# First loads, low weight bits on ScalarE, and the place of W's products in a fused attention, MoE and MLP kernel

## The chip, the cores and the metric

The kernel runs on one core of one Trainium2 chip. The metric is the device time of one execution in microseconds (us), lower is better; the kernel before was run three times. The engines are TensorE (PE; its weight loads are listed as PEld), VectorE (DVE), ScalarE (ACT), GpSimd (POOL) and SyncE (SP), which here issues most DMAs.

## The reference

Three stages follow each other; shapes are in brackets.

```python
# 1. linear attention with decay, per head [4 batches, 8 heads, 768 steps, 48 dims]
for t in range(S):
    cur   = einsum('bhd,bhe->bhde', u * k_t, v_t)
    y_t   = einsum('bhd,bhde->bhe', r_t, state + cur)
    state = w * state + einsum('bhd,bhe->bhde', k_t, v_t)
# 2. x = y as [3072, 384]; top-1 mixture of 8 experts with a skip score
xc = x[x @ w_skip > 0];  e = argmax(xc @ w_gate);  g = softmax(xc @ w_gate)[e]
x[those rows] = xc + g * (relu(xc @ w1[e]) @ w2[e])          # w1 [384, 1024], w2 [1024, 384]
# 3. second MLP
out = (((x @ m1) * (x @ m2)) @ w3) @ w_out                   # m1, m2 [384, 1024], w3 [1024, 1024], w_out [1024, 384]
```

Stage 3 uses one matrix W = w3 @ w_out, computed once, so that only one product is left after `(x @ m1) * (x @ m2)`. The weights of stage 3 arrive as 64-bit floats.

## The kernel before, in words

**Attention.** The 768 steps are cut into 12 chunks of 64, and the heads of two pairs of batches give 24 tiles `n` (chunk `n // 2`, pair `n % 2`) of 128 partitions. A tile needs two loads: `TB` (`load_t`, r and k transposed, 512 KB) and `KV` (`load_v`, r, k and v, 576 KB). `TB` has three buffers, `KV` two for each pair. Per tile:

- `prep` (line 359, DVE) multiplies `TB` by tables of powers of w and gives `FK`;
- `scores` (line 371, PE, 32 products of 48 rows and 64 columns into the one bank `sc`); `evac` (line 376, DVE) masks them into `Fs`;
- `prep_k` (line 383, POOL) gives `kd` and waits for `prep` of the tile after; `prep_m` (lines 389 and 390, POOL) gives r·u·k, `bonus` (line 395, DVE) sums it and `prep_v` (line 405, ACT, 8 instructions) multiplies v by it;
- `y_mm` (lines 425 and 428, PE, 32 + 32 products of 64 or 48 rows); `x_out` (line 446, DVE) adds the bonus and stores the tile to memory;
- `ds_mm` (line 441, PE, 32 products) adds to the state `S` in PSUM; `state_copy` (lines 413 and 415, DVE and ACT) scales it and copies it to SBUF;
- `x_trans` (line 457) and `logits` (line 470), PE, full array, feed the router, whose steps `route_a` to `route_d` and `place` run on DVE for groups of tiles; `place_mm` (line 599) is PE.

The order is written out by hand: everything from line 733 on is emitted in program order on each engine's queue, and no planner moves it. The loop at line 772 does, for n = 0 to 21: `load_t(n+4)`, `prep(n+2)`, `state_copy(n+1)`, `scores(n+1)`, `prep_k(n+1)`, `prep_m(n+2)`, `evac(n+1)`, `bonus(n+1)`, `y_mm(n)`, logits and transposes of earlier tiles, `x_out(n)`, `ds_mm(n)`, `place_mm`, `load_v(n+4)`, `place`. After it a tail of eleven steps finishes tiles 22 and 23 and the router, gathers the rows of the first expert (`load_x`, line 863) and transposes them (`trans_x`).

**W between the tiles.** The products of W are 64 (8 blocks `f` by 8 `g`, `w_mm`, line 696), each one fp32 product of 128 by 128 by 384, shown in the trace as two instructions of line 708. `keep(k)` takes one product for each 4 units of `k` if its weights are ready; if none is, each 2 units cost one `idle_mm`, two dummy products of bf16 (`DQ` = 256 columns). `WK[n]` gives the units at two places: the first before was after `y_mm`, the second after `x_trans` and `prep_v`, ahead of `ds_mm`. In the tail `TK`, `TQ` and `KW` give them, and the last line of it runs what is left:

```python
        trans_x(0)
        while n_w[0] < NF:
            keep(1)
```

**The weights of W.** `jobs` (line 273) are 12 raw loads of 768 or 1024 KB (`load_w`, three buffers). Each is narrowed from 64 to 32 bits: `magnitude` (line 105, ACT), then `shift` (line 113), `low` (line 116) and `sign` (line 120), all DVE. `w_step` takes the next of these three; `WN[n]` says how many at each of three places in an iteration. A block is usable after three calls of `w_ready`. The first three raw loads are issued ahead of the loop, among `load_v(2)`, `load_v(3)` and `load_t(3)`.

Stages 2 and 3 (from line 908 and line 1082) are not touched.

Of the kernel before, what the change touches and what calls it, by code (L numbers as in the profile page):

```python
# [8 lines left out]
F32 = mybir.dt.float32  # L9
F32R = mybir.dt.float32r  # L10
BF16 = mybir.dt.bfloat16
I32 = mybir.dt.int32
AF = mybir.ActivationFunctionType
ALU = mybir.AluOpType
# [17 lines left out]
BIG = 1.0e6  # L32
WLO, WHI = 0.5, 1.5
DQ = 256
NM, NW = 10, 9
# [7 lines left out]
W3B = 5  # L43
WK = [(1, 1)] * 9 + [(1, 2)] * 13
WN = [(0, 0, 0)] * 2 + [(1, 1, 1)] * 5 + [(1, 0, 1)] * 15
KW = 16
# [13 lines left out]
def fused_kernel(ctx, tc, att, kv, wt, u, wg, we, w3, wo, w12, r, k, v, wu, out):  # L60
# [46 lines left out]

    def narrow(raw, t):

        wl, wh = raw[:, :, 0], raw[:, :, 1]  # L110

        def shift():
            nc.vector.tensor_scalar(out=t, in0=t, scalar1=3, scalar2=None, op0=ALU.logical_shift_left)

        def low():
            nc.vector.scalar_tensor_tensor(out=t, in0=wl, scalar=29, in1=t,
                                           op0=ALU.logical_shift_right, op1=ALU.bitwise_or)

        def sign():
            nc.vector.scalar_tensor_tensor(out=t, in0=wh, scalar=-0x80000000, in1=t,  # L120
                                           op0=ALU.bitwise_and, op1=ALU.bitwise_or)

        return [shift, low, sign]

# [101 lines left out]
    with tc.manual_schedule():  # L226
# [10 lines left out]
        def load_t(n):  # L237
            nc.sync.dma_start(out=TB[n % 3].rearrange("p a h t -> p (a h t)"), in_=att[n])
# [21 lines left out]
        load_t(1)  # L260
        nc.sync.dma_start(out=un.rearrange("p h d -> p (h d)"), in_=u.to_broadcast([P, D]))
        load_v(0)
        load_v(1)
        load_t(2)
        nc.gpsimd.memset(ident, 0.0)
        nc.gpsimd.affine_select(out=ident, in_=ident, compare_op=ALU.not_equal, fill=1.0, base=0,
# [33 lines left out]
        nc.vector.tensor_tensor(out=UT[:, 0, 0], in0=Ur, in1=cb, op=ALU.mult)  # L300
        SB = [ps_s.tile([P, 512], F32, tag=f"S{bp}", name=f"S{bp}") for bp in range(2)]
        S = [b[:, 0:D].rearrange("p (h d) -> p h d", h=NH) for b in SB]

        half = [slice(64 * q, 64 * q + 64) for q in range(2)]
# [79 lines left out]

        def prep_m(n):

            c, bp = divmod(n, 2)
            m = P_[n] = wk.tile([P, NH, HD], F32, name="m")
            first = nc.gpsimd.tensor_tensor(out=m, in0=KV[bp][c % 2][:, 0], in1=un, op=ALU.mult)
            nc.gpsimd.tensor_tensor(out=m, in0=KV[bp][c % 2][:, 1], in1=m, op=ALU.mult)  # L390
            return first
# [167 lines left out]
        found, pend = [], []  # L559
        SL = [b[:, 384:464] for b in SB]  # L560
        for b in SL:
            nc.vector.memset(b, 0.0)
        slots = wk.tile([P, 80], F32, name="slots", bufs=1)
# [72 lines left out]
        w3_ = {}  # L636

        done, fresh = set(), [[], [], []]
        n_w = [0]

        def w_steps():


            def front(i):
# [11 lines left out]
                if wide:  # L656
                    magnitude(raw, x.bitcast(I32))
                    return narrow(raw, x.bitcast(I32))
                return [lambda: nc.scalar.copy(out=x, in_=raw)]

            ops = None
            for i, job in enumerate(jobs):
# [5 lines left out]
                for k, op in enumerate(now):  # L668
                    op()
                    if k + 1 == len(now):  # L670
                        load_w(i + 3)
                        fresh[-1].append(job)
                    if ops is None:
                        ops = front(i + 1)
                    yield
# [58 lines left out]
        table_k(0)  # L734
        load_t(3)
        nc.vector.tensor_tensor(out=UT[:, 1, 1], in0=Tk, in1=cb, op=ALU.mult)
        prep(1)
        sc = scores(0)
        prep_m(0)
        table_k(1)  # L740
        prep_k(0)
        evac(0, sc)
        bonus(0)
        prep_m(1)
        for bp in range(2):
            nc.vector.memset(S[bp], 0.0)
        nc.vector.tensor_tensor(out=w128, in0=pw[:, 5], in1=pw[:, 5], op=ALU.mult)
        prep_v(0)
        more_consts = consts()
        load_w(0)  # L750
        load_v(2)
        load_v(3)
        nc.sync.dma_start(out=wgs, in_=wg)
        load_w(1)
        load_w(2)
        todo = []
# [15 lines left out]
        for n in range(NT - 2):  # L772
# [13 lines left out]
            if n == NT - 3:  # L786
                bonus(NT - 1)
            next(more_consts, None)
            w_step(WN[n][0])
            w_ready()  # L790
            y_mm(n)
            keep(4 * WK[n][0])
            run_todo()
            if n > 0:
                x_trans(n - 1)
            prep_v(n + 1)
            keep(4 * WK[n][1])
            w_step(WN[n][1])
            w_evac(0)
            x_out(n)  # L800
            ds_mm(n)
            place_mm(n % 2)
            if n + 4 < NT:
                load_v(n + 4)
            if n < NT - 3:
                place(3)
# [36 lines left out]
        nc.vector.tensor_tensor(out=fb[:, 0:8], in0=wc, in1=wtt, op=ALU.not_equal)  # L843
        nc.vector.tensor_copy(fb[:, 8:16], acc)
    actx.close()

# [567 lines left out]
def _layout(i):  # L1414
# [20 lines left out]
    def words(a):  # L1435
# [11 lines left out]
        "wt": wt,  # L1447
        "u": c(u.reshape(1, D)),
        "wg": c(wg.reshape(ND, P, 9).transpose(1, 0, 2)),
# [23 lines left out]
```

## Time and profile before

| | us |
|---|---|
| median of 3 runs (lowest, highest) | 633.9 (633.12, 634.04) |
| the profiled execution | 637.01 |
| its span in the trace | 635.3 |
| PE busy, share of the span | 614.5, 97% |
| DVE busy, share of the span | 464.1, 73% |
| ACT busy, share of the span | 290.7, 46% |
| POOL busy, share of the span | 141.3, 22% |

The table gives busy time over the whole span, in which three stages with different limits lie one after the other; attention and the products of W end at about 184 us. A busy PE is not PE at its peak: an instruction that waits for its weights or runs at half clock counts as busy. In rows of the trace, times are from the span's start, "x32" counts instructions, and "[2.24 <-DVE ...]" is idle time of the engine ahead of the row and who ended it.

### The profile page before, as it was taken

Reading aid. Unit: us, or ns where it says so; the run is one execution under the profiler, and the core shown is the slowest. Engines: PE = TensorE matmul, PEld = TensorE weight load, DVE = VectorE, ACT = ScalarE, POOL = GpSimd, SP = SyncE. Lnnn points to the kernel's source line nnn. Section 1 sums busy time; section 2 is a strip of 40 time slices with the busy share of each in tenths; the row PEclk is TensorE's granted clock in tenths of the full one; section 3 lists DMA queues with packets and bytes.
Section 4 is the critical chain, followed back from the end, with each engine's and each line's share of the span. In section 5 each row is a group of like instructions: output and inputs, shape, how many; then the busy total and the mean of one; then the engine's idle time right before and its main releaser. Section 6 shows DMA issues by size and latency. Waiting matters only on the chain.

```text
span 635.3 us, 15258 instructions
## 1 busy us (share of the span) xinstructions
PE 614.5 (97%) x6313; PEld 545.4 (86%) x6313; DVE 464.1 (73%) x820; ACT 290.7 (46%) x705; POOL 141.3 (22%) x140
## 2 busy tenths in 40 slices
PE   7999998999999999999998999999999999999996
PEld 6888877888769999989997989988988988988985
DVE  7699998986477799999956954863863863863760
ACT  2555644534355667666534542443443442442430
POOL 3856465463040232232132300000000000000000
PEclk9799998999999999999999999999999999999999
DMA  8889988575148768877321002002002002000001
GB/s 310 358 280 378 326 291 286 177 252 198 45 127 301 277 230 296 287 241 272 112 75 57 1 17 84 1 18 83 2 18 84 1 17 84 2 18 33 1 2 55
DMA packets 26941, 90.40 MB, mean 142 GB/s; under 512 B 4009, under 2 KB 10729, under 8 KB 25840
## 3 DMA queue, kind: packets, MB, share of 16 engines
q1 hardware_dynamic: 24816, 84.11, 38.1%
q0 software_dynamic: 2048, 5.24, 2.5%
q8 instruction: 51, 0.84, 0.5%
q14 instruction: 26, 0.21, 0.1%
HBM read 77.61 MB, written 12.39 MB: 142 GB/s over the span
## 4 chain that ended last, share of the span: by engine, by line
PE 78%; DVE 11%; DMA 5%; issue 3%; ACT 1%; SPq 0%; POOL 0%; DVEq 0%; ACTq 0%
PE po L1237 16%; PE xy L1196 11%; PE za L1196 10%; PE zb L1196 8%; PE wp L708 6%; PE hp L923 6%; PE y L942 5%; DMA TB<-in_att 3%; DVE elo L87 3%; PE sc L371 3%; PE S L441 2%; PE y L425 2%; PE y L428 1%; PE G L428 1%; DVE hl L927 1%
## 5 line engine op out<-in xcount | busy, mean ns | idle before, releaser
L1178 DVE TENSOR_TENSOR C<-st,za 128x512 f32<-128x512 f32 x47 | 32.3, 687 | 69.7 <-ACT st L1213 69.6
L87 DVE TENSOR_TENSOR elo<-raw,ehi 128x768 fp32r<-128x768 f32 x64 | 60.4, 948 | 4.1 <-ACT ehi L86 4.0
L1237 PE MATMUL po<-pl,W_hi 128*128 128x512 f32 (+1 forms) x152 | 58.1, 383 | 0.0
L1237 PE MATMUL po<-ph,W_hi 128*128 128x512 f32 (+1 forms) x152 | 58.0, 382 | 0.0
L1237 PE MATMUL po<-ph,W_lo 128*128 128x512 f32 (+1 forms) x152 | 57.6, 379 | 0.0
L923 PE MATMUL hp<-xh,ehi 128*128 128x240 f32 x192 | 54.5, 286 | 3.0 <-DVE hl L927 2.4
L1213 ACT COPY st<-xy 128x256 f32<-128x256 f32 x47 | 17.6, 374 | 81.8 <-PE xy L1196 81.8
L86 ACT CAST ehi<-raw 128x768 fp32r<-128x768 f32 x64 | 52.7, 829 | 2.1 <-DMA raw<-in_we 2.1
L1196 PE MATMUL xy<-bxh,w12h 128*128 128x256 f32 x188 | 53.3, 283 | 0.0
L1196 PE MATMUL xy<-bxl,w12h 128*128 128x256 f32 x188 | 53.1, 282 | 0.0
L1196 PE MATMUL xy<-bxh,w12l 128*128 128x256 f32 x188 | 53.1, 282 | 0.0
L923 PE MATMUL hp<-xl,ehi 128*128 128x240 f32 x192 | 52.6, 276 | 0.0
L923 PE MATMUL hp<-xh,elo 128*128 128x240 f32 x192 | 52.4, 274 | 0.0
L708 PE MATMUL wp<-wo_s,w 128*128 128x384 f32 x128 | 51.7, 515 | 0.1
L405 ACT ACTIVATE zv<-KV,z 128x48 f32<-128x48 f32 x184 | 44.0, 327 | 8.0 <-DVE z L395 6.9
L1196 PE MATMUL za<-bxh,w12l 128*128 128x512 f32 x141 | 45.1, 320 | 0.0
L1196 PE MATMUL za<-bxh,w12h 128*128 128x512 f32 x141 | 45.0, 319 | 0.0
L1196 PE MATMUL za<-bxl,w12h 128*128 128x512 f32 x141 | 44.7, 317 | 0.0
L942 PE MATMUL y<-ehi,hh 128*128 128x384 f32 (+1 forms) x128 | 43.3, 339 | 0.0
L942 PE MATMUL y<-elo,hh 128*128 128x384 f32 (+1 forms) x128 | 43.2, 338 | 0.0
L942 PE MATMUL y<-ehi,hl 128*128 128x384 f32 (+1 forms) x128 | 43.1, 337 | 0.0
L923 PEld LDWEIGHTS hp<-xh,ehi 128*128 128x128 f32 x192 | 36.1, 189 | 7.9 <-DVE hl L927 6.9
(249 smaller groups left out, 1671.5 us busy)
## 6 DMA issues: line engine op xcount, KB each, us to landing
raw<-in_we SPq DMA_DIRECT2D x32, 768.0 KB, 5.1
KV<-in_kv SPq DMA_DIRECT2D x24, 576.0 KB, 5.3
TB<-in_att SPq DMA_DIRECT2D x24, 512.0 KB, 7.3
raww<-in_w SPq DMA_DIRECT2D x8, 1024.0 KB, 7.5
raw<-in_w SPq DMA_DIRECT2D x8, 768.0 KB, 6.6
xm<-xg SPq DMA_DIRECT2D x48, 96.0 KB, 3.3
out<-ob SPq DMA_DIRECT2D x17, 256.0 KB, 2.0
x<-xm SPq DMA_DIRECT2D x20, 192.0 KB, 2.8
```

The source lines that it names most:

```text
L86: nc.scalar.copy(out=hi, in_=raw)
L87: (eng or nc.vector).tensor_tensor(out=lo, in0=raw, in1=hi.bitcast(F32), op=ALU.subtract)
L371: nc.tensor.matmul(sc[m, h], FK[d, 1, h], FK[d, 0, h], start=True, stop=True)
L405: nc.scalar.activation(out=zv[:, h], in_=v[:, h], func=AF.Copy, scale=z[:, h:h + 1])
L425: nc.tensor.matmul(yv[m, h], Fs[m, h], v[m, h], start=(h == 0), stop=True, skip_group_check=True)
L708: nc.tensor.matmul(ps, w3[:, g], wo_s[:, g], start=(g == 0), stop=(g == NF - 1))
L923: nc.tensor.matmul(hp, a, b, start=(i == 0), stop=(i == 8))
L942: nc.tensor.matmul(ys[e, t], a[:, P * t:P * t + ROWS[t]], b[:, D:2 * D], start=(f == 0 and i == 0), stop=(f == NF - 1 and i == 2))
L1178: nc.vector.tensor_tensor(out=halves(C[:, 0]), in0=st[:, 0:2], in1=halves(za), op=ALU.add)
L1196: nc.tensor.matmul(o, a, m, start=first and i == 0, stop=(i == 2), skip_group_check=True)
L1213: nc.scalar.copy(out=st[:, 0], in_=X)
L1237: nc.tensor.matmul(po, a[:, f, c], b[:, t], start=(i == 0), stop=(i == 3 * NF - 1))
```

## The change

- **Loads.** `u` is stored 128 times in memory and loaded without a broadcast. `load_v(2)` comes right after `load_t(2)`, `load_v(3)` after `load_t(3)`. The three first raw loads of W leave the start: `load_w(0)`, `(1)` and `(2)` are issued in iterations 1, 2 and 3, after `load_v(n+4)`.
- **Start.** The two PSUM memsets of the state and of the slots become one per bank, at the very start. `prep_m(0)` moves from POOL to DVE, behind `evac(0)`. The constants of the router (`consts`) start at n = 2 and not at n = 0.
- **Low bits.** For W's weights `shift` and `low` are replaced: `ahead` (ACT) turns the low word, read as an unsigned integer, into the three low bits in a tile `bits`; `join` (DVE) shifts and ors in one instruction. `sign` stays. The next job's `magnitude` is issued after a job's last step and not after its first. The weights of stage 3's other matrices (`prep_steps`) keep the three DVE steps.
- **W's steps and products.** `WN` gives no step before n = 3, one at n = 3 and two per iteration from n = 4. The first place of `keep` moves ahead of `y_mm`, directly behind `scores(n+1)`; the second behind `ds_mm` and `place_mm`, directly ahead of the next `scores`. `WK` gives 4 and 0 units for n = 0 to 8, 4 and 4 for n = 9 and 10, 8 and 8 from n = 11.

```diff
-WK = [(1, 1)] * 9 + [(1, 2)] * 13
-WN = [(0, 0, 0)] * 2 + [(1, 1, 1)] * 5 + [(1, 0, 1)] * 15
+WK = [(1, 0)] * 9 + [(1, 1)] * 2 + [(2, 2)] * 11
+WN = [(0, 0, 0)] * 3 + [(0, 0, 1)] + [(1, 0, 1)] * 18
+LW = (1, 2, 3)
...
-        return [shift, low, sign]
+        def ahead():
+            nc.scalar.activation(out=bits, in_=wl.bitcast(U32), func=AF.Copy, scale=LOW[0], bias=LOW[1])
+
+        def join():
+            nc.vector.scalar_tensor_tensor(out=t, in0=t, scalar=3, in1=bits,
+                                           op0=ALU.logical_shift_left, op1=ALU.bitwise_or)
+
+        return [shift, low, sign] if bits is None else [ahead, join, sign]
...
-        nc.sync.dma_start(out=un.rearrange("p h d -> p (h d)"), in_=u.to_broadcast([P, D]))
+        nc.sync.dma_start(out=un.rearrange("p h d -> p (h d)"), in_=u)
         load_v(0)
         load_v(1)
         load_t(2)
+        load_v(2)
+        SB = [ps_s.tile([P, 512], F32, tag=f"S{bp}", name=f"S{bp}") for bp in range(2)]
...
+        for b in SB:
+            nc.vector.memset(b[:, 0:464], 0.0)
...
-                    if ops is None:
+                    if ops is None and k + 1 == len(now):
                         ops = front(i + 1)
...
         load_t(3)
+        load_v(3)
         nc.vector.tensor_tensor(out=UT[:, 1, 1], in0=Tk, in1=cb, op=ALU.mult)
         prep(1)
         sc = scores(0)
-        prep_m(0)
         table_k(1)
         prep_k(0)
         evac(0, sc)
+        prep_m(0, nc.vector)
         bonus(0)
         prep_m(1)
-        for bp in range(2):
-            nc.vector.memset(S[bp], 0.0)
...
-        load_w(0)
-        load_v(2)
-        load_v(3)
         nc.sync.dma_start(out=wgs, in_=wg)
-        load_w(1)
-        load_w(2)
...
-            next(more_consts, None)
+            if n > 1:
+                next(more_consts, None)
             w_step(WN[n][0])
             w_ready()
+            keep(4 * WK[n][0])
             y_mm(n)
-            keep(4 * WK[n][0])
             run_todo()
             if n > 0:
                 x_trans(n - 1)
             prep_v(n + 1)
-            keep(4 * WK[n][1])
             w_step(WN[n][1])
             w_evac(0)
             x_out(n)
             ds_mm(n)
             place_mm(n % 2)
+            keep(4 * WK[n][1])
             if n + 4 < NT:
                 load_v(n + 4)
+            if n in LW:
+                load_w(n - LW[0])
...
-        "u": c(u.reshape(1, D)),
+        "u": c(np.broadcast_to(u.reshape(1, D), (P, D))),
```

## Rows read from the trace of the kernel before

**Rows 1.** Windows: stretch, its length, busy us of each engine, clock, DMA share, GB/s.
```profile
6.00:7.00 1.00, 1.00 (x16) 0.69 (x16) 0.98 (x4) 0.00 (x0) 0.00 (x0) 1.00 0.76 118
...
17.00:18.00 1.00, 1.00 (x25) 1.00 (x24) 1.00 (x2) 1.00 (x5) 0.00 (x0) 0.50 1.14 451
```

**Rows 2.** Chain that ended last, first 50 us: start, us, what.
```profile
3.62 10.10 DMA TB<-in_att
...
13.79 11.31 DMA TB<-in_att
```

**Rows 3.** Timeline, the start: start, us, engine, line, operation, count, idle before.
```profile
2.43 0.17 DVE L289 TENSOR_SCALAR wc<-wtt 128x8 f32<-128x8 f32 x1 [1.33 <-DMA wtt<-in_wt]
...
13.82 2.02 DVE L359 TENSOR_TENSOR FK<-TB,UT 128x1024 f32<-128x1024 f32 x1
```

**Rows 4.** Timeline: scores of tiles 2, 3, 4, 7, 8, 17, 18 and 23.
```profile
16.50 1.89 PE L371 MATMUL sc<-FK 48*64 48x64 f32 x32 [2.23 <-DVE Fs L376]
...
23.64 1.11 PE L371 MATMUL sc<-FK 48*64 48x64 f32 x32
...
29.22 1.11 PE L371 MATMUL sc<-FK 48*64 48x64 f32 x32
...
47.36 1.11 PE L371 MATMUL sc<-FK 48*64 48x64 f32 x32
...
53.45 1.11 PE L371 MATMUL sc<-FK 48*64 48x64 f32 x32
...
119.17 1.11 PE L371 MATMUL sc<-FK 48*64 48x64 f32 x32
...
125.90 1.11 PE L371 MATMUL sc<-FK 48*64 48x64 f32 x32
...
160.70 1.15 PE L371 MATMUL sc<-FK 48*64 48x64 f32 x32
```

**Rows 5.** Timeline of PE and of its weight loads in iteration 16.
```profile
120.11 1.09 PE L425 MATMUL y<-KV,Fs 64*64 64x48 f32 x32
121.03 1.10 PE L428 MATMUL y<-Ss,FK 48*64 48x48 f32 x32
122.06 0.91 PE L708 MATMUL wp<-wo_s,w 128*128 128x384 f32 x2
122.81 0.73 PE L470 MATMUL y<-wgs,xT 128*128 128x9 f32 x6
...
123.76 1.46 PE L708 MATMUL wp<-wo_s,w 128*128 128x384 f32 x4
125.14 0.92 PE L441 MATMUL S<-KV,kd 64*48 64x48 f32 x32
...
125.14 0.80 PEld L441 LDWEIGHTS S<-KV,kd 64*48 64x48 f32 x32 [0.55 <-issue]
```

**Rows 6.** Timeline, end of iteration 11: state products, placement, scores.
```profile
86.74 0.92 PE L441 MATMUL S<-KV,kd 64*48 64x48 f32 x32
87.60 0.28 PE L599 MATMUL S<-s_v,s_oh 128*128 128x80 bf16 x3
87.81 1.15 PE L371 MATMUL sc<-FK 48*64 48x64 f32 x32
```

**Rows 7.** Iteration 13: PE's stop (timeline), and the clock behind it (windows).
```profile
99.79 0.37 PE L428 MATMUL G<-Ss,FK 48*64 48x48 f32 x5 [1.80 <-issue]
...
102.00:104.40 2.40, 2.40 (x6) 0.76 (x6) 2.40 (x3) 2.33 (x10) 0.85 (x1) 0.50 1.02 394
```

**Rows 8.** One line of code each: durations min/median/max in ns, first and last start.
```profile
L105 ACT ACTIVATE w<-raww x8: 1135/1168/1190, 25.1 to 112.9; 128x1024 f32<-128x1024 f32 x8
...
L120 DVE SCALAR_TENSOR_TENSOR w<-raww,w x8: 1207/1396/1737, 37.5 to 129.5; 128x1024 int32<-128x1024 int32 x8
```

**Rows 9.** Timeline: the first expert's second transpose and its first product.
```profile
184.17 0.48 PE L875 MATMUL pT<-ident,xr 112*128 112x112 f32 x3 [0.50 <-DMA xr<-xm,sidx]
...
185.17 0.61 PE L923 MATMUL hp<-xh,ehi 128*128 128x240 f32 x3 [0.31 <-ACT xh L876]
```

More of the change, by code (lines that the diff above doesn't have):

```diff
@@ L12 @@
 I32 = mybir.dt.int32
+U32 = mybir.dt.uint32
 AF = mybir.ActivationFunctionType
@@ L33 @@
 WLO, WHI = 0.5, 1.5
+LOW = (2.0 ** -29 * (1 - 2.0 ** -16), 1.14e-4 - 0.5)
 DQ = 256
@@ L106, in magnitude, with narrow @@
         return t
-    def narrow(raw, t):
+    def narrow(raw, t, bits=None):
         wl, wh = raw[:, :, 0], raw[:, :, 1]
@@ L264, in fused_kernel @@
         load_t(2)
+        load_v(2)
+        SB = [ps_s.tile([P, 512], F32, tag=f"S{bp}", name=f"S{bp}") for bp in range(2)]
+        S = [b[:, 0:D].rearrange("p (h d) -> p h d", h=NH) for b in SB]
+        SL = [b[:, 384:464] for b in SB]
+        for b in SB:
+            nc.vector.memset(b[:, 0:464], 0.0)
         nc.gpsimd.memset(ident, 0.0)
@@ L300, in fused_kernel @@
         nc.vector.tensor_tensor(out=UT[:, 0, 0], in0=Ur, in1=cb, op=ALU.mult)
-        SB = [ps_s.tile([P, 512], F32, tag=f"S{bp}", name=f"S{bp}") for bp in range(2)]
-        S = [b[:, 0:D].rearrange("p (h d) -> p h d", h=NH) for b in SB]
         half = [slice(64 * q, 64 * q + 64) for q in range(2)]
@@ L383, in prep_k, with prep_m @@
                 return nc.gpsimd.tensor_tensor(out=kd, in0=KV[bp][c % 2][:, 1], in1=KU[:, c % 2], op=ALU.mult)
-        def prep_m(n):
+        def prep_m(n, eng=nc.gpsimd):
             c, bp = divmod(n, 2)
             m = P_[n] = wk.tile([P, NH, HD], F32, name="m")
-            first = nc.gpsimd.tensor_tensor(out=m, in0=KV[bp][c % 2][:, 0], in1=un, op=ALU.mult)
-            nc.gpsimd.tensor_tensor(out=m, in0=KV[bp][c % 2][:, 1], in1=m, op=ALU.mult)
+            first = eng.tensor_tensor(out=m, in0=KV[bp][c % 2][:, 0], in1=un, op=ALU.mult)
+            eng.tensor_tensor(out=m, in0=KV[bp][c % 2][:, 1], in1=m, op=ALU.mult)
             return first
@@ L559, in fused_kernel @@
         found, pend = [], []
-        SL = [b[:, 384:464] for b in SB]
-        for b in SL:
-            nc.vector.memset(b, 0.0)
         slots = wk.tile([P, 80], F32, name="slots", bufs=1)
@@ L636, in fused_kernel @@
         w3_ = {}
+        bits = ac.tile([P, NF * P], I32, name="bits")
         done, fresh = set(), [[], [], []]
@@ L657, in front @@
                     magnitude(raw, x.bitcast(I32))
-                    return narrow(raw, x.bitcast(I32))
+                    return narrow(raw, x.bitcast(I32), bits[:, 0:x.shape[1]])
                 return [lambda: nc.scalar.copy(out=x, in_=raw)]
@@ L844, in fused_kernel @@
         nc.vector.tensor_copy(fb[:, 8:16], acc)
+        assert next(wprep, True)
     actx.close()
```

## The prediction

> **What bounds the kernel now.** The page's busy shares (the table above) name PE, but over three stages together, and the change touches only the first. So I read on in this order. The windows show how each stretch of attention runs; the chain of waits says who holds the end; the timeline of PE gives the price of each part of an iteration.
>
> In the chain the first 25 us are two loads of `TB` in a row, 10.10 us and 11.31 us from issue to landing [rows 2]. The first holds `prep(2)` until 13.82 us [rows 3], and PE has stood idle for 2.23 us when the scores of tile 2 begin at 16.50 us [rows 4]. Then PE runs at half of its 2.4 GHz, 0.50 granted at 17 us [rows 1], and the next iteration takes 23.64 − 16.50 = 7.14 us [rows 4].
>
> From there PE is the bound. An iteration with 8 dummies takes 29.22 − 23.64 = 5.58 us, one with two products of W 53.45 − 47.36 = 6.09, one with three 125.90 − 119.17 = 6.73 [rows 4], and in the last PE has no gap that a wait explains. So a product costs 6.73 − 6.09 = 0.64 us, an iteration without any 6.09 − 1.28 = 4.81, and a dummy (5.58 − 4.81) / 8 = 0.10.
>
> The twenty iterations from 2 to 21 lie between 23.64 and 160.70 us: 137.06 us [rows 4]. Three with dummies (16.7), four with two products (24.4), thirteen with three (87.5) and five insertions of placement products at 0.31 (1.6, below) make 130.2. The other 6.9 us are losses: the largest in iteration 13, where PE stops for 1.80 us in the middle of 32 products without a wait that the profile shows, and then runs at half clock, 0.50 over 2.4 us and more [rows 7]; together some 3.7 us. Some 0.5 of the rest I give to the router's products, which stay.
>
> **The change part by part.**
>
> **Start.** Ahead of `TB` of tile 2 the same bytes are queued as before, but `u` comes without its broadcast; in the second in which that load was in flight the DMA moved 118 GB/s at a busy share of 0.76 [rows 1], against 451 later. I let tile 2 land 1.1 us earlier, at 12.6 (bounds: not at all, and 2.4 us). `prep(2)` took 2.02 us [rows 3] beside POOL's `prep_m(1)`; POOL has less to do ahead of it now, and I take 0.8 off (bounds 0 and 0.8). That puts the scores of tile 2 at 14.6. `TB` of tile 4, the second long load, has two KV and one TB left ahead of it and no raw load, so it leaves the chain; what is late next is PE itself. Iteration 1 has no second half of `y_mm` (0.92) and no logits (0.6 of the 0.95 us that these and the transposes take from 122.81 to 123.76 [rows 5]): 4.81 − 1.5 plus 4 dummies (0.4) and their switch (0.25) is 4.0, if the clock holds. The scores of tile 3 begin at 18.6 and not 23.64: −5.0 us. Bounds: −6.2 (tile 2 at 13.4) and −2.1 (half clock again, 7.1 us for that iteration).
>
> The memsets of the state banks go to where DVE waits 1.33 us for its first load [rows 3], and hide there; without that cover they cost at most 1 us. `prep_m(0)` on DVE, two operations, ends before `TB` of tile 2 lands, and DVE waited for that load anyway: nothing. The stores of tile 0 and `load_v(4)` stand behind fewer loads on SP, and `load_w(0..2)` pass into the queue ahead of `TB` of tiles 6 to 8, which are wanted two iterations (11 us) later; nothing, and 1 to 2 us if the queue is full.
>
> **Switches on PE.** In rows 5 scores, `y_mm` and `ds_mm` use tiles of 64 columns, products of W, logits and transposes the whole array. Before, all of the latter lay together: one switch to the whole array and one back per iteration. After the second half of `y_mm` the next 64-column group would start 0.92 us on (120.11 to 121.03), but W starts after 1.03; this single product holds PE for 0.75, not 0.64; the two after the transposes, with the switch back, take 1.38, not 1.28 [rows 5]. So a pair of switches costs 0.11 + 0.11 + 0.10 = 0.32 us around W. Placement between state products and scores shows the same: 1.07 us from 86.74 to 87.81 [rows 6] against 0.76 from 125.14 to 125.90 [rows 4, 5], 0.31 with three short products in it; I take 0.25 for the switches alone, and for dummies too.
>
> Now W stands between scores and `y_mm` and between state products and scores, inside the 64-column run. Counting from iteration 2: the first place adds a pair in each of 20 iterations, the second in the 13 from n = 9. W's weights come later: by the steps and the three calls of `w_ready` the first product is possible at n = 7, none at n = 11, two at n = 12, and four per iteration from n = 13. So 25 of these pairs hold products (8.0 us) and 8 dummies (2.0); five merge with placement (−1.25): +8.75. No trace of before has scores directly ahead of W; per W pair I keep 0.15 and 0.36 as ends, ±4 us in all.
>
> That a switch has such a price agrees with the Trainium skill, "TensorEngine Tiling (Array Packing)", Key Properties: changing the tiling mode drains the engine. Against it stands "TensorE: Matmul & The Clock Gate", Part 3, where PE pulls weight loads ahead of products in flight if their row groups differ; by that rule the new places would cost nearly nothing, and the sum would be 8.75 lower. The trace speaks for the drain: at the switch back the weight loads have been idle for 0.55 us and the first load starts with the first product, both at 125.14 [rows 5].
>
> **Products and dummies.** 44 products in the loop and not 47: −1.9. The three run behind the first expert's transposes, where PE waits 185.17 − 184.65 = 0.52 us anyway [rows 9]: 1.9 − 0.5 = +1.4. From iteration 2 there are 44 dummies and not 24 (4 each for n = 2 to 6, 16 and 8 for n = 11 and 12): +2.0.
>
> **Weights.** DVE loses one of three operations per block; `join` should take about what `sign` takes, 1.40 us [rows 8] (ends 1.2 and 1.9). ACT gains `ahead`, by the nearest row, `magnitude`, 1.17 us [rows 8] (ends 0.7 and 1.9), 12 times. Both engines work beside a PE that is the bound: nothing on the path. If DVE is late, scores wait for `evac`; DVE's lighter load is what makes early iterations safe. `magnitude` now comes three iterations after its load is issued, so that ACT waits for no raw load.
>
> **Losses.** Of the 6.9 us, 0.5 of the router stays and I keep 0.8 for new stops of PE; a run of small products is now broken up by W, which should make them rarer: −5.6.
>
> **Sum**, against the profiled execution (637.01, a span of 635.3 and 1.7 around it): −5.0 + 8.75 − 1.9 + 1.4 + 2.0 − 5.6 = −0.35, that is 636.7. But the median is 633.9, 3.1 lower than the profiled one, about the size of the loss in iteration 13. Whether runs without the profile have that stop isn't known; I count half of it, 1.85, as not there to be won. Against the median: −0.35 + 1.85 = +1.5, so 635.4.
>
> **The rivals.**
>
> 1. *The clock falls again in the gap before the scores of tile 2.* Now PE ends the state products of tile 0 at about 13.1 and waits 1.5 us, before 2.23. For it: it fell then. Against it: the gap is shorter. Iteration 1 takes 7.1 and not 4.0: +2.9 with less around it, 638.3.
> 2. *The switches cost half (the other side: faster).* In the new places either the switch in or the switch back overlaps with work in flight; per W pair 0.16, per dummy pair 0.12: −4.0 and −1.0, so 630.5. It is faster than before by the measurable 0.2% from a W pair below 0.23 us on. For it: neither new place is in the trace. Against it: all three switches that are there cost the same.
> 3. *Runs without the profile have the stop of iteration 13 too*, and all of it is won: 1.85 less, 633.6, no difference. For it: runs agree within 0.15%; against it: the 3.1 us between profile and median.
> 4. *Weight loads are pulled ahead after all*: 635.4 − 8.75 = 626.7. The 0.55 us idle speaks against it.
> 5. *The loads come no earlier*: tile 2 lands at 13.7 as before; +1.1, 636.5, within the forecast's own range.
>
> **How the numbers follow.** My forecast, a start won and spent again on switches, 0.48, its own range 633.4 to 637.5; rival 1 0.15; rival 2 0.18; rival 3 0.13; rival 4 0.03; rival 5 0.03. For 8 in 10 the range takes most of rivals 1 and 2: 630.6 to 639.0. This kernel can tell about 0.2%, 1.3 us, from no change. Faster by more: rival 2 (0.17), 4 (0.03), a third of rival 3 (0.04), the low end of the forecast (0.06): 0.30. Within: 0.16 of the forecast, 0.09 of rival 3 and 0.01 of rival 2: 0.26. Slower: the rest, 0.44.
>
> **What would show it.** Right: scores of tile 3 near 18.6 us at full clock, iterations 13 to 21 at 6.73 + 0.64 + 2 × 0.32 = 8.0 us, scores of tile 23 near 159 us, the first expert's product 1 to 2 us further behind its transpose. Rival 1 shows half clock between 15 and 22 us, rival 2 iterations of 7.7 or less with the weight loads of `y_mm` starting before W ends. Wrong: if DVE or ACT ends the waits of PE from iteration 4 on, or if raw loads hold `prep`.

## The result, and the profile after

The change makes the kernel slower: a median of 639.81 us in six runs, 633.50 before beside it, a ratio of 1.0113 with a 95% interval of 1.0078 to 1.0148. The six runs go from 639.33 to 659.94 us; the longest, in which the granted clock was lower (0.96 in the mean), is left out of the ratio. The prediction was 635.4 us: the direction is right, the size is not. The profiled execution took 639.33 us (span 637.6), that of before 637.01 (635.3).

The page of the kernel after, busy time by engine, answers to the table of before: PE has 4.8 us more, DVE 12.4 less, ACT 11.2 more.

```profile
PE 619.3 (97%) x6325; PEld 544.2 (85%) x6325; DVE 451.7 (71%) x808; ACT 301.9 (47%) x717; POOL 135.7 (21%) x138
```

The start, in the timeline of after and, below it, its DMA issues (the last number is us from issue to landing), against [rows 2, 3, 4]. `TB` of tile 2 is issued at 3.92 us and lands 7.7 us later, at 11.6, before at 13.72. But `prep(2)` doesn't start then: DVE is busy with `prep_m(0)` and what follows it until 12.76. The scores of tiles 2 and 3 begin at 14.63 and 18.55 us (forecast 14.6 and 18.6).

```profile
3.92 0.45 SPq L248 DMA_DIRECT2D TB<-in_att  x1
...
9.53 1.08 DVE L402 TENSOR_TENSOR m<-KV,un 128x384 f32<-128x384 f32 x1
10.64 1.32 DVE L403 TENSOR_TENSOR m<-KV,m 128x384 f32<-128x384 f32 x1
11.99 0.55 DVE L408 TENSOR_REDUCE z<-m 128x8 f32<-128x384 f32 x1
...
12.76 1.21 DVE L372 TENSOR_TENSOR FK<-TB,UT 128x1024 f32<-128x1024 f32 x1
...
14.63 1.15 PE L384 MATMUL sc<-FK 48*64 48x64 f32 x32 [1.49 <-DVE Fs L389]
18.55 1.11 PE L384 MATMUL sc<-FK 48*64 48x64 f32 x32
```

```profile
TB<-in_att SPq DMA_DIRECT2D x1, 512.0 KB, 7.7
```

An iteration of after with four products, in the timeline of PE and its weight loads, against [rows 5]. W (L719) now stands ahead of `y_mm` (L438) and ahead of `scores` (L384), and at each return to the 64-column groups the weight loads have been idle for 0.55 us. The wait that the row at 129.06 names (`w` by DVE, the `join` at 127.68) was over at 128.90; the same 0.55 stands at 131.63 without a releaser.

```profile
127.68 1.22 DVE L130 SCALAR_TENSOR_TENSOR w<-w,bits 128x1024 int32<-128x1024 int32 x1
...
129.06 1.01 PEld L384 LDWEIGHTS sc<-FK 48*64 48x64 f32 x32 [0.55 <-DVE w L130]
129.07 1.15 PE L384 MATMUL sc<-FK 48*64 48x64 f32 x32
...
130.14 1.56 PE L719 MATMUL wp<-wo_s,w 128*128 128x384 f32 x4
131.63 1.01 PEld L438 LDWEIGHTS y<-KV,Fs 64*64 64x64 f32 x32 [0.55 <-issue]
...
145.38 1.15 PE L384 MATMUL sc<-FK 48*64 48x64 f32 x32
153.43 1.15 PE L384 MATMUL sc<-FK 48*64 48x64 f32 x32
161.57 1.15 PE L384 MATMUL sc<-FK 48*64 48x64 f32 x32
```

Iteration 20 takes 153.43 − 145.38 = 8.05 us (forecast 8.0), but the scores of tile 23 begin at 161.57 and not near 159. In the tail three products (six instructions of L719) and two dummies stand behind the second transpose, and the first expert starts at 187.60; before at 185.17 [rows 9].

```profile
185.19 0.48 PE L884 MATMUL pT<-ident,xr 112*128 112x112 f32 x3 [0.66 <-DMA xr<-xm,sidx]
185.51 2.11 PE L719 MATMUL wp<-wo_s,w 128*128 128x384 f32 x6
187.46 0.38 PE L265 MATMUL G<-zb 128*128 128x256 bf16 x2
187.60 0.58 PE L932 MATMUL hp<-xh,ehi 128*128 128x240 f32 x3
```

The two scores of the start, the late iterations and the tail come out as forecast, and still the sum is off. That was the question for the runs.

### The profile page after: what moved, and what is told of

The parts are those of the page before. It is cut to its first block, busy times and chain, and to the rows that moved or that the text cites. A ratio compares the mean times of both kernels' runs of the same rounds, so it can differ in the third digit from the quotient of the medians.

```text
span 637.6 us, 15263 instructions
## 1 busy us (share of the span) xinstructions
PE 619.3 (97%) x6325; PEld 544.2 (85%) x6325; DVE 451.7 (71%) x808; ACT 301.9 (47%) x717; POOL 135.7 (21%) x138
## 4 chain that ended last, share of the span: by engine, by line
PE 83%; DVE 11%; issue 3%; ACT 1%; DMA 1%; POOL 0%; DVEq 0%; ACTq 0%
PE po L1246 16%; PE xy L1205 11%; PE za L1205 10%; PE zb L1205 8%; PE wp L719 6%; PE hp L932 6%; PE y L951 5%; PE sc L384 4%; DVE elo L90 3%; PE S L454 3%; PE y L438 2%; PE G L438 2%; PE y L441 2%; PE G L483 2%; PE G L441 1%
## 5 line engine op out<-in xcount | busy, mean ns | idle before, releaser
L719 PE MATMUL wp<-wo_s,w 128*128 128x384 f32 x128 | 49.9, 510 | 0.0
```

The source lines that it names most:

```text
L719: nc.tensor.matmul(ps, w3[:, g], wo_s[:, g], start=(g == 0), stop=(g == NF - 1))
```

## The experiments

Sixteen runs in four groups, of fourteen new kernels and of before and after once more; each is compared with runs of before on its own chip (medians 634.59, 633.65, 633.74 and 633.65 us). Kernels are compared with each other by these ratios.

### Before, once more

The kernel before, unchanged. 

> The kernel before, unchanged, for a second trace. Theory (the stop of PE in iteration 13 is an accident of one execution): no stop over 1 us in the loop, scores of tile 23 near 157 us and not 160.7, span 631.5 to 632.5. Rival (the stop belongs to the kernel and the profile slows everything evenly): a stop of 1 to 2 us in iteration 13 again, scores of tile 23 at 160 to 161.

It took 633.01 us with a span of 631.3, 4.0 us less than the profiled execution on which the forecast rests. Its timeline, against [rows 4] (the scores of tiles 3, 4, 14, 15 and 23), and the window of [rows 7], where the clock (the 0.50 of [rows 7]) now is 1.00:

```profile
21.67 1.11 PE L371 MATMUL sc<-FK 48*64 48x64 f32 x32
27.38 1.18 PE L371 MATMUL sc<-FK 48*64 48x64 f32 x32
...
94.76 1.15 PE L371 MATMUL sc<-FK 48*64 48x64 f32 x32
...
101.61 1.11 PE L371 MATMUL sc<-FK 48*64 48x64 f32 x32
...
156.78 1.15 PE L371 MATMUL sc<-FK 48*64 48x64 f32 x32
```

```profile
102.00:104.40 2.40, 2.40 (x90) 2.40 (x84) 2.40 (x2) 0.55 (x3) 1.57 (x1) 1.00 1.04 360
```

There is no stop in iteration 13 (101.61 − 94.76 = 6.85 us, not 10.4), and tile 3 starts at 21.67 and not 23.64. The 4 us were accidents of one execution: 1.97 at the start, 1.95 from there to tile 23 (a smaller loss elsewhere takes back part of the stop).

### After, once more

The kernel after, unchanged. 

> The changed kernel once more, unchanged. Theory (the price of the switches is fixed, PE's stops without a wait in the early iterations are accidents of one execution): iterations 13 to 21 take 8.04 to 8.23 us again, the scores of tile 3 begin at 18.4 to 18.8 us again, but the stops among iterations 2 to 12 lie elsewhere or have other lengths; a span of 636 to 640. Rival (the stops belong to the program): they lie in iterations 9 and 12 again, with the same lengths to 0.2 us.

640.11 us, span 638.3. Tile 3 at 18.2, iterations 13 to 21 at 8.04 to 8.23 again. Of the two stops without a wait in after, that of 0.51 us at 35.65 is there again (at 35.51), the 0.84 us at 62.80 is gone, and one of 0.69 stands at 45.72. Behind it the granted clock falls to 0.50 (the number ahead of the DMA share), and iterations 6 and 7 take 6.62 and 7.12 us, not 5.87 and 5.78. So some stops move between executions, and the price of the late iterations doesn't.

```profile
47.60:50.80 3.20, 3.20 (x52) 2.66 (x46) 2.20 (x4) 3.10 (x12) 2.05 (x3) 0.50 0.94 306
```

### The places of W

Three kernels move `keep`, and nothing else.

`old_places`, on after (`before_new_places` is the reverse, on before):

```diff
-            keep(4 * WK[n][0])
             y_mm(n)
+            keep(4 * WK[n][0])
...
             prep_v(n + 1)
+            keep(4 * WK[n][1])
...
             place_mm(n % 2)
-            keep(4 * WK[n][1])
```

`one_place`, on after:

```diff
-WK = [(1, 0)] * 9 + [(1, 1)] * 2 + [(2, 2)] * 11
+WK = [(0, 1)] * 9 + [(0, 2)] * 2 + [(0, 4)] * 11
```

> The changed kernel with both places of W's products where they were before (after y_mm, and ahead of ds_mm), counts WK and everything else as changed. Switch theory: 25 pairs around products at 0.36 us, 8 around dummies at 0.25, less 1.25 for placement: 9.5 us less than the changed kernel, 630.3; iterations 15 to 21 at 7.4 and not 8.1 us; weight loads of W's second product no longer idle for 0.55 us ahead of them. Rival (late weights, dummies, ScalarE or stops of PE cost the time): 637 to 640.

> The changed kernel with all units of WK at its second new place (between state products and scores), none at the first. Switch theory: 20 pairs go at the first place (14 products, 6 dummies), 7 come at the second for n = 2 to 8; 13 pairs less, some 4.5 us less than the changed kernel: 635.3; iterations 15 to 21 at 7.75 us. Rival (the place between scores and y_mm hides something that y_mm waits for): no less, or more, than 639.8.

> The kernel before with nothing but the two places of W's products moved to the new ones (WK, WN, loads and weights as before). Switch theory: 34 pairs around products at 0.36 and 8 around dummies at 0.25 from iteration 1 on, less 1.25 for five placements and less up to 2 us where DVE was the bound in iterations 4 to 8: +11, 644.5 (642 to 646). Rival (half-priced or hidden switches): 636 to 640.

The same iteration (20) in `old_places`, `one_place` and `before_new_places`, its own scores' start and the next one's:

```profile
141.90 1.11 PE L384 MATMUL sc<-FK 48*64 48x64 f32 x32
149.28 1.11 PE L384 MATMUL sc<-FK 48*64 48x64 f32 x32
```

```profile
147.42 1.15 PE L384 MATMUL sc<-FK 48*64 48x64 f32 x32
155.13 1.15 PE L384 MATMUL sc<-FK 48*64 48x64 f32 x32
```

```profile
150.46 1.15 PE L371 MATMUL sc<-FK 48*64 48x64 f32 x32
157.86 1.15 PE L371 MATMUL sc<-FK 48*64 48x64 f32 x32
```

With four products 7.38 us at the old places, 7.71 at one new one, 8.05 at two: 0.33 and 0.34 per pair of switches. With before's three products 7.40, and 6.74 in the same iteration of before: 0.33 per pair again. The price is settled, and it was forecast (0.32). In time: `before_new_places` 642.94 us, ratio 1.0131 (1.0097 to 1.0164), within what was expected. But `old_places` took 637.60, 1.0036 (1.0001 to 1.0070), and `one_place` 640.56, 1.0091 (1.0057 to 1.0125), 7.3 and 5.3 us above what the switch theory gave; both times are the rivals'. In the profiled executions the iterations 13 to 21 of `old_places` take 5.3 us less than those of after (67.76 against 73.02), but its iterations 2 to 12, where switches were taken out too, 1.4 more (71.35 against 70.00). In `old_places` PE stops without a wait five times in iterations 3 to 8, longest

```profile
56.31 0.90 PE L441 MATMUL y<-Ss,FK 48*64 48x48 f32 x22 [1.56 <-issue]
```

and behind it the granted clock is 0.50, the lower of the two levels (its windows, the number ahead of the DMA share):

```profile
56.00:58.00 2.00, 1.69 (x24) 1.36 (x25) 1.73 (x5) 0.34 (x2) 1.01 (x2) 0.90 0.84 258
58.00:60.00 2.00, 2.00 (x10) 1.61 (x8) 0.51 (x2) 0.00 (x0) 0.00 (x0) 0.50 0.89 305
```

### New places early, old ones late

On after, and likewise the second `keep`:

```diff
-            keep(4 * WK[n][0])
+            if n < 13:
+                keep(4 * WK[n][0])
             y_mm(n)
+            if n >= 13:
+                keep(4 * WK[n][0])
```

> The changed kernel, with W's products at the old places from n = 13 on (iterations with four products) and at the new ones before. Switch theory: 18 pairs less at 0.335, 1 back where placement had merged: 6 us less than the changed kernel, 633.5 to 634.5; iterations 13 to 21 at 7.4 us. Stops: none more than in the changed kernel, since nothing is changed up to n = 12. Rival (the scatter of old_places comes from iterations 13 to 21): 636 or more.

636.65 us, 1.0032 (0.9999 to 1.0065); the profiled execution 634.08, 5.3 less than after's, with late iterations of 7.38 to 7.73. So the late iterations give back what the switches cost there. The median is 2.2 us above the expected range and in that of the rival (636 or more), in runs that scatter from 634.1 to 640.2 (one of 651.9); by the ratios it is 0.8% or 5.1 us below after, where 6 were expected. The scatter isn't in iterations 13 to 21 of the one profile, as the rival has it; where it is in the other runs, no trace shows.

### The start without the rest, and low bits on DVE

`start_only` is before with the change's loads, memsets, `prep_m(0)` and `consts`, and

```diff
-        load_w(0)
...
-        load_w(1)
-        load_w(2)
...
                 load_v(n + 4)
+            if n < 3:
+                load_w(n)
```

> The kernel before with the start of the changed one alone: u without broadcast, load_v(2) and load_v(3) early, memsets of the state first, prep_m(0) on DVE, constants from n = 2, and the three first raw loads issued in iterations 0, 1 and 2. Places, WK, WN and the three DVE steps as before. Start theory: scores of tile 3 near 18.5 us against 21.7 to 23.6; of that 2 to 3 us are left at the end, since DVE and PE's instruction supply bound iterations 3 to 9: 630 to 632 where the kernel before has 633.5. Rival (nothing is left, the early iterations only wait longer): 633 to 634.

637.25 us, 1.0034 (1.0004 to 1.0064): theory and rival both miss. Tile 3 at 18.3, but iteration 3 takes 11.57 us. ACT's `magnitude` waits for a raw load, `xT` behind it on ACT's queue is late, and PE waits for `xT`:

```profile
30.17 1.14 ACT L105 ACTIVATE w<-raww 128x1024 f32<-128x1024 f32 x1 [4.90 <-DMA raww<-in_w]
...
31.21 0.46 ACT L462 COPY xT<-T 128x384 f32<-128x384 f32 x1
...
31.72 0.60 PE L473 MATMUL G<-wgs,xT 128*128 128x9 f32 x2 [3.74 <-ACT xT L462]
```

So the change needs its later steps of W once the raw loads come later. `dve_low_bits` is after with

```diff
-                    return narrow(raw, x.bitcast(I32), bits[:, 0:x.shape[1]])
+                    return narrow(raw, x.bitcast(I32))
```

> The changed kernel with the low bits of W's weights on DVE again (shift, low, sign), everything else as changed. Theory (both engines work beside PE, the edit is worth nothing): within 1 us of the changed kernel, 639 to 641. Rival (ScalarE's added work costs, or DVE's saved work pays): 2 us or more away from it.

645.56 us in four runs (642.76 to 656.60), 1.0152 (1.0081 to 1.0223). The time is the rival's, but the interval overlaps after's, and the late iterations are after's; the profiled execution loses 4.6 us in iterations 6 and 7, at a stop of 1.88 us (it ends at 46.75) that no wait explains and the lower clock behind it. That ACT's share helps is thus not shown by itself.

### Where the start's gain goes: DMA

`old_places_few_loads` is `old_places` reading only two of the twelve raw blocks of W, used for all:

```diff
                 kind, q = jobs[i]
+                if kind in first_w:
+                    raw_w.append(first_w[kind])
+                    return
```

> The run old_places with two raw loads of W only: every block is narrowed from the first load of its kind, so W is not the reference's; instructions of all engines but the DMA issues stay. Theory (PE's stops without a wait are its instruction blocks arriving late because data transfers fill the DMA engines in the first 60 us): no stop over 0.5 us in iterations 3 to 9, scores of tile 14 at 80 to 83 us against 89.2, time 626 to 629. Rival (the stops come from the instruction stream itself, whatever the DMA does): stops as in old_places, scores of tile 14 at 87 to 91, time 633 to 639.

632.96 us, 1.0003 (0.9968 to 1.0038), by the ratios 0.33% or 2.1 us below `old_places`, which the intervals don't separate. The theory fails: four stops of 0.53 to 1.39 us are left, iterations 3, 7 and 9 are still long, and tile 14 begins at 86.19. Then the larger stream was taken away, from `old_places` and from after:

```diff
         def load_t(n):
+            if 5 <= n <= 13:
+                return
...
         def load_v(n):
+            if 5 <= n <= 13:
+                return
```

> The changed kernel with W's products at the places of before, and without the loads of tiles 5 to 13 (TB and KV): these tiles are computed from the data of earlier ones, so the output is another. The work of every engine stays. Theory A (data in the DMA queues delays PE's instruction blocks): the stops without a wait in iterations 3, 8 and 9 go, iterations 2 to 9 take 5.2 to 6.1 us, the scores of tile 14 begin at 84 and not 89.2, the median is 632. Theory B (PE uses up its instructions faster than they come, whatever else moves): stops of 1 us and more stay among iterations 2 to 9, tile 14 at 87 to 89, the median 635.5 to 637.5.

> The changed kernel without the loads of tiles 5 to 13 (they are computed from the data of earlier tiles, so the output is another). Theory (the traffic of DMA, not the places of W, is what lengthens the iterations before tile 14): iterations 2 to 9 lose what is above 5.5 us, the scores of tile 14 begin at 84 to 85 and not at 88.5, iterations 13 to 21 stay at 8.04 to 8.23, the median is 636. Rival (the early iterations of the changed kernel are bound by PE and DVE): tile 14 at 87.5 to 88.5, the median 639.

`old_places_no_tiles`: 628.26 us, 0.9916 (0.9887 to 0.9946), by the ratios 1.2% or 7.6 us below `old_places`; iterations 2 to 6 take 5.14 or 5.15 us each, one stop of 1.40 is left at 58.35. `after_no_tiles`: 636.72, 1.0057 (1.0039 to 1.0074), 0.56% or 3.5 us below after, no stop between 15 and 100 us. Its windows, and ahead of them those of after, then of the second execution of before (the last two numbers are the busy share of DMA and GB/s):

```profile
20.00:60.00 40.00, 39.30 (x981) 34.79 (x979) 31.71 (x46) 25.93 (x86) 29.93 (x37) 1.00 0.96 363
```

```profile
20.00:60.00 40.00, 40.00 (x1011) 35.40 (x1011) 33.27 (x48) 27.46 (x89) 30.88 (x38) 1.00 0.57 175
```

```profile
20.00:60.00 40.00, 38.09 (x909) 33.58 (x909) 35.85 (x44) 22.40 (x71) 26.35 (x36) 0.99 0.89 327
```

DMA is busy 0.96 of these 40 us and not 0.89. From 10 to 20 us it is the other way round, 0.91 against 1.03: the first raw loads of W, which the change takes out of the start, and the tiles, which follow each other sooner, now fall into this stretch. Without the tiles' loads it is 0.57, and PE is busy in 40.00 of 40. The timeline of `after_no_tiles` (tiles 3, 4, 5, 14 and 23) shows what the other engines alone need, 5.48 us for each of the iterations 2 to 6; after's 2 to 8 take 5.49 to 6.25, and its iteration 9 takes 7.94 against 6.90.

```profile
18.24 1.11 PE L388 MATMUL sc<-FK 48*64 48x64 f32 x32
23.72 1.11 PE L388 MATMUL sc<-FK 48*64 48x64 f32 x32
29.21 1.11 PE L388 MATMUL sc<-FK 48*64 48x64 f32 x32
...
85.67 1.15 PE L388 MATMUL sc<-FK 48*64 48x64 f32 x32
...
158.69 1.15 PE L388 MATMUL sc<-FK 48*64 48x64 f32 x32
```

From tile 3 to tile 23 that is 140.45 us; after takes 161.57 − 18.55 = 143.02.

### Smaller parts on the kernel before

`u_alone`, on before:

```diff
-        nc.sync.dma_start(out=un.rearrange("p h d -> p (h d)"), in_=u.to_broadcast([P, D]))
+        nc.sync.dma_start(out=un.rearrange("p h d -> p (h d)"), in_=u)
...
-        "u": c(u.reshape(1, D)),
+        "u": c(np.broadcast_to(u.reshape(1, D), (P, D))),
```

`start_raw_early` is `start_only` with the three raw loads where they were, `u_low_bits` is `u_alone` with `ahead` and `join` of the change, and `u_even` is `u_low_bits` with

```diff
-WK = [(1, 1)] * 9 + [(1, 2)] * 13
-WN = [(0, 0, 0)] * 2 + [(1, 1, 1)] * 5 + [(1, 0, 1)] * 15
+WK = [(0, 0)] * 6 + [(0, 1)] * 2 + [(0, 2)] * 3 + [(0, 0)] + [(0, 4)] * 9 + [(0, 3)]
+WN = [(0, 0, 0)] * 2 + [(1, 0, 1)] * 20
```

> The kernel before, with u loaded without its broadcast and nothing else. Theory (the broadcast holds up the loads queued behind it): the scores of tile 2 begin about 1 us earlier than the 16.0 of the second execution of before, those of tile 3 near 20.5 and not 21.7, and nothing else moves; the median is 1 us lower, 632.5. Rival (what is won at the start is lost again in stops of PE in the early iterations, as in the kernel with the start alone): tile 3 near 20.5, tile 14 at 94.8 or later, the median 633.5 to 637.

> The kernel before with the new start (u without its broadcast, load_v(2) and load_v(3) early, the memsets and prep_m(0) moved), but with the three raw loads of W ahead of the loop, where they were. Theory (the DMA engines are full from 10 us on, so that whatever comes earlier makes something else later): the scores of tile 3 begin near 18.5 us, but the TB of tile 4, behind the raw loads, lands no earlier than before, the scores of tile 4 at 26 to 27.4 (27.4 in the second execution of before), the median is 632.5 to 633.7. Rival (the start's gain is kept when ACT waits for no raw load): tile 4 at 24, the median 630.5.

> The kernel before with u loaded without its broadcast, and the low bits of W's weights by ACT (ahead and join in the place of shift and low), with the same number of steps at the same places. Theory (DVE is busy all the time from 25 to 60 us and ends waits of PE of 0.7 and 1.5 us there, so each us that it saves there counts): DVE saves some 0.8 us per job, the waits of scores on evac shrink, iterations 3 to 6 are shorter by 0.5 each, the median is 630.5 to 631.5. Rival (DMA sets the pace of the early iterations): no change against u alone, 632.5.

> As u_low_bits, but with two steps of W's weights per iteration from n = 2 and not three in iterations 2 to 6, so that a raw load of W comes every one and a half iterations, and with W's products at the second place of before, 1 to 2 per iteration up to n = 10 and then 4, without a dummy in the loop. Theory (DMA and DVE are overloaded in iterations 2 to 9, and PE has to wait for them): less load there, the median 0.5 to 1.5 us under u_low_bits. Rival (what PE doesn't do early it must do late, and the early iterations stop at the same blocks): the same as u_low_bits or up to 2 us more.

| kernel | median us | ratio (95%) |
|---|---|---|
| u_alone | 632.51 | 0.9983 (0.9967 to 0.9998) |
| start_raw_early | 632.96 | 0.9990 (0.9963 to 1.0017) |
| u_low_bits | 631.92 | 0.9988 (0.9956 to 1.0021) |
| u_even | 637.03 | 1.0048 (1.0016 to 1.0080) |

`u_alone` is the one kernel with the right output that beats before by more than its interval; but that ends at 0.9998, and of eleven such kernels one may do so by chance. Its profiled execution (636.04 us) has the rival's sign instead: a stop of 1.02 us ends at 56.22, the clock falls behind it, and tile 14 begins at 97.51. `start_raw_early` shows where more of the start goes: tile 3 begins at 18.29, and tile 4 only at 26.45; in the second execution of before, which started 3.4 us later, at 27.38. Two things hold it: `prep(4)` waits for the `TB` behind the raw loads, and `evac(3)`, next on DVE, frees the bank `sc` only at 25.84; PE itself, after stops of 1.53 and 0.62 us without a wait, is through with tile 2 at 26.45.

```profile
24.02 1.23 DVE L362 TENSOR_TENSOR FK<-TB,UT 128x1024 f32<-128x1024 f32 x1 [5.41 <-DMA TB<-in_att]
```

```profile
20.52 0.62 PE L374 MATMUL sc<-FK 48*64 48x64 f32 x14 [1.53 <-issue]
...
26.45 0.20 PE L444 MATMUL S<-KV,kd 64*48 64x48 f32 x1 [0.62 <-issue]
26.45 1.15 PE L374 MATMUL sc<-FK 48*64 48x64 f32 x32
```

`u_low_bits` can't be told from `u_alone`. `u_even`, 5 us above `u_low_bits`, misses both of what was expected and refutes the idea that a thinner load early is enough: the clock is at 0.50 from 42.4 to 52.4 us, and its iteration 12 holds a stop of 1.63 us, then runs at a mean clock of 0.76 from 88 to 95 us and takes 11.24 us where the next takes 7.42. In the stretch of that stop DMA was full (1.02):

```profile
84.00:87.40 3.40, 1.79 (x56) 1.55 (x51) 3.40 (x6) 1.99 (x11) 0.44 (x1) 1.00 1.02 407
```

The stop that is left in `old_places_no_tiles` (it ends at 58.35) seems to speak against DMA as the cause, with a share of 0.12 beside it. But the instruction packet ahead of it (see the last section) starts at 55.87, and just before that stretch DMA was busy at 0.90:

```profile
53.00:55.00 2.00, 2.00 (x47) 1.76 (x47) 1.93 (x6) 1.30 (x2) 1.92 (x3) 1.00 0.90 360
55.00:58.35 3.35, 1.95 (x68) 1.83 (x65) 3.25 (x7) 2.38 (x12) 0.87 (x1) 1.00 0.12 45
```

### A balanced version

After with its start and low bits, the first place kept up to n = 6, W at before's second place from n = 7, and

```diff
-WK = [(1, 0)] * 9 + [(1, 1)] * 2 + [(2, 2)] * 11
-WN = [(0, 0, 0)] * 3 + [(0, 0, 1)] + [(1, 0, 1)] * 18
+WK = [(1, 0)] * 7 + [(0, 1)] * 2 + [(0, 2)] * 2 + [(0, 0)] + [(0, 5)] + [(0, 4)] * 9
+WN = [(0, 0, 0)] * 3 + [(0, 0, 1)] + [(1, 0, 1)] * 3 + [(1, 1, 1)] * 6 + [(1, 0, 1)] * 9
```

> The changed kernel with its start, its low bits and its dummies up to iteration 6, but W's products at the second place of before from iteration 7, one third step of W's weights in iterations 7 to 12, no dummies from iteration 7 on, and 47 products in the loop (1, 1, 2, 2, 0, 5, then 4 each), so that none is left behind the first expert's transposes. Theory (the sum of PE's work decides, and the change lost on switches, dummies and the tail what it won at the start): against the changed kernel 20 W pairs at 0.335, 24 dummies at 0.1 and 1.8 in the tail, less 1.9 for three products, -9 us in the span: 628.5; the median 632, 0 to 2 us below before, the rest going to stops in the early iterations. Rival (the loop is held elsewhere once PE has less to do): iterations 13 to 21 longer than 7.4 us by waits on DVE or ACT, the median 635 or more.

634.21 us, 1.0008 (0.9980 to 1.0036), no difference from before, 2.2 us above the expected 632, and by the ratios 1% below after. Iterations 13 to 21 are at 7.38 to 7.73 as the theory wants; tile 14 begins only at 90.3, behind three stops of 0.68 to 0.88 us between 35 and 52, a clock of 0.50 from 52.4 to 59 us, and an iteration 12 of 9.21 us, in which PE waits 0.68 us for DVE. The gain of the start is spent in the early iterations.

## Why the prediction was wrong

**Start: the number right, by luck in part.** Both scores came within 0.05 us of the forecast, and rivals 1 and 5 are out (clock 1.00 from 12 to 20 us; the load came earlier). But two terms were wrong and cancel: the load of tile 2 came 2.1 us earlier and not 1.1, and `prep_m(0)` on DVE, put at nothing because DVE would wait for that load anyway, holds `prep(2)` for 1.1 us after the landing. And the −5.0 counts from a start that other executions don't have: against the second one it is 21.67 − 18.55 = −3.1.

**Switches: right.** 0.33 per pair was measured in three pairs of kernels, 0.32 forecast. Around dummies it is 0.34 and not 0.25 (iterations 2 to 6 take 5.48 us in `after_no_tiles` and 5.14 in `old_places_no_tiles`), 0.7 us for the eight of them. Rivals 2 and 4 fall with it; rival 4 was weak from the start, since a product of W takes the whole array, 128 by 128 [rows 5], so that no load behind it has row groups of its own.

**Products, tail, dummies: right.** From tile 23's scores to the first expert, after takes 187.60 − 161.57 = 26.03 us and the second execution of before 181.28 − 156.78 = 24.50: +1.5, forecast +1.4. An early iteration without disturbance takes 5.48; 4.81, four dummies (0.4) and their switch (0.25) make 5.46, though the switch took 0.34 and the rest 5.14, not 5.21.

**Low bits: right that nothing on the path waits for them.** PE has no gap between 15 and 100 us in `after_no_tiles`. On 128 by 1024, `ahead` took 1.16 us and `join` 1.22 (median), forecast 1.17 and 1.40.

**Losses: this step failed**, "Of the 6.9 us, 0.5 of the router stays and I keep 0.8 for new stops of PE ...: −5.6". From tile 3 to tile 23 the forecast is 137.06 + 8.75 − 1.9 + 2.0 − 5.6 = 140.3; after takes 143.02, 2.7 more, and 144.23 in its second execution. `after_no_tiles` takes 140.45: without the tiles' loads the forecast holds to 0.15 us, by luck in part, since 0.8 of it was kept for stops, and this run has none. So the losses that I took away came back as other ones, where DMA is fuller (0.96 against 0.89), all in iterations 3 to 9: 2.6 us that go when the tiles' loads go, 1.35 of them in the two stops. I had named PE as what is late next and had no row on how full DMA was between 18 and 102 us. That W between the small products makes stops rarer may be: up to 65 us after has two of 0.4 us and more in each of its two executions, `old_places` five and `old_places_few_loads` four; these few executions are not enough to show it.

**The baseline: the same step, second half.** "I count half of it, 1.85, as not there to be won." All of it wasn't there, and part of the start's gain neither: the profiled execution lay 637.01 − 633.50 = 3.5 us above the median, so 1.65 was missing. 2.7 + 1.65 = 4.35, and the miss is 639.81 − 635.4 = 4.4. Rival 3, that runs without the profile hold the stop of iteration 13 too, was wrong in the other direction: the second execution, which doesn't hold it, lies at the median.

**Where the time went**, after against the second execution of before, by the scores' starts: 88.55 − 94.76 = −6.2 up to tile 14 (3.1 of it up to tile 3, and with 12 products of W fewer by then), 73.0 − 62.0 = +11.0 from tile 14 to 23 (nine of those products and two pairs of switches in each iteration), +1.5 in the tail with the other three: +6.3, the difference of the spans (637.6 − 631.3).

The stops have a likely cause, and part of it is open. The Trainium skill, "Runtime: NRT & Kernel Launch", Instruction fetch mechanics, has instructions come by DMA in blocks of 16 KiB, 256 instructions, and calls the cost of a new block mostly hidden. The trace agrees with the blocks, and not with hidden: every stop lies at a point of the program that returns each 256 instructions, behind a packet of the instruction queue (below). That PE waits there for a late block is the reading that fits them all; no run held back a block by itself. Data traffic makes blocks later: of those fetched between 20 and 65 us, the packets of after start 2.2 to 3.3 us before PE comes to the block (mean 2.5), those of the second execution of before 2.4 to 4.9 (mean 3.2), those of `after_no_tiles` 3.2 to 6.2 (mean 4.6), one execution each. Full DMA engines alone don't make a block late: from 106.6 to 108.6 us of after they are busy at 1.01, and the packet that starts then comes 7 us ahead of PE. Why a block is late in one execution and not in the next, no run here tells.

## What to carry to other kernels

Profile the kernel before twice: a loss that the second execution doesn't have can't be won, and a sum made against the first one starts too high. Before loads are moved forward, read the busy share of DMA in the stretch behind them: where it is near 1, what comes earlier may only make something else late. And keep work of another tiling of the array together; each separate place costs a pair of switches, here 0.33 us, twenty times over.

## What the hardware showed

- PE stops without a wait in the trace, mostly in the middle of a run of small products: 45 stops of 0.4 to 2.4 us in the eighteen traces. Each ended 2.15 to 2.53 us after the start of a packet on the queue q8, as here the window from 60.0 to 60.5 us of after (queue and kind, packets, MB, share) and the stop in its timeline. The packet took 0.9 to 1.1 us each time; it came late, not slowly. Over the whole of after q8 moved 51 packets (0.84 MB); PE has 2 × 6,325 products and weight loads, one packet for each 248. With the instructions of PE's own queue counted too (67 in after), PE stood at each of the 45 stops 193 or 194 instructions beyond a multiple of 256. Which of these points stop, and for how long, differs between executions.

```profile
q8 instruction: 1, 0.02, 11.2%
```

```profile
62.80 0.26 PE L438 MATMUL G<-KV,Fs 64*64 64x48 f32 x3 [0.84 <-issue]
```

- Behind some stops the granted clock fell to the lower of its two levels (1.2 GHz) for a while: those of 0.69 us (after, second execution), 1.02 (`u_alone`), 1.56, 1.63 and 1.80. Behind others it stayed at 1.00: 0.84, 1.40 (`old_places_no_tiles`), 1.53 (`start_raw_early`) and 2.42 us (`start_only`). So the length of the stop alone doesn't decide it. Stop and slow clock together cost iteration 12 of `u_even` 11.24 − 7.42 = 3.8 us.
- Loading `u` by a broadcast of one row held up what was queued beside it: from 6 to 7 us DMA moved 111 GB/s with it (second execution of before) and 313 GB/s without (`u_alone`). The medians differ by 1.2 us, just clear of their interval.
